# Replanning the opening of an attention and gated-linear-unit kernel: two load queues, weights first, single-step narrowing, two gates off VectorE

## The chip, the cores and the metric

The kernel runs on one core of a Trainium2 chip. The metric is the device time of one execution in microseconds, as the median of several runs. A profiled execution also gives a span, which is shorter than the time of that same execution by a constant 1.8 us; marks inside an execution are given on the span's clock. All comparisons are between runs that were classed as fast, unless it is said.

## The reference, cut to what matters

```python
kv  = einsum('bhsd,bhse->bhde', k, v)            # 8 batches, 8 heads, 576 rows, 64 wide
out = einsum('bhsd,bhde->bhse', q, kv)
x   = out / sqrt(mean(out*out, -1) + 1e-6) * g_norm    # then (B, S, 512)
gate = sigmoid(causal_conv(x, conv_w))           # 5 taps over time, per channel
val  = x @ w_val                                 # weights are float64 in the input
result = (gate * val) @ w_out
```

The weights arrive as 64-bit floats and have to be narrowed to 32 bits on the core. That costs seven VectorE instructions for each of eight blocks (four of `w_val`, four of `w_out`).

## The kernel before

Everything is emitted by steps with a planned time. The plan only sorts the steps. Each engine then runs its own instructions in that order and waits where data is missing. All large loads go through the sync queue (SP). An engine *issues* a load by an instruction of its own, and the load *lands* later.

```python
def raw_product(b, c):                   # one chunk of up to 128 rows, 5 chunks per batch
    raw = ps("raw", [P, C], ...)         # two PSUM banks
    ...
def scales(b, c):
    nc.vector.reduce_sum(out=ss, in_=sq.rearrange("p (h e) -> p h e", h=H), axis=AX.X)
    nc.gpsimd.tensor_scalar(out=ss, in0=ss, scalar1=D * EPS, ..., op0=ALU.add)
    nc.gpsimd.tensor_tensor(out=rt, in0=ss, in1=mhalf, op=ALU.pow)
def normalise(b, c):                     # x = raw * rt, frees the raw bank
    nc.vector.tensor_tensor(out=x, in0=raw, in1=rt, op=ALU.mult)
def gate_tap(b, jt, tap):                # 4 a gate, 4 gates a batch
    nc.vector.scalar_tensor_tensor(out=gate, in0=xT[shifted], scalar=cwT[...], in1=gate, ...)
def narrow(key, dst):                    # seven VectorE instructions in one go
    ...
# ---- plan of the opening (cut) ----
at(0.0, load_kv, 0, 0);  at(0.1, load_kv, 0, 1)      # k, v of batch 0
at(0.2, load_q_rows, 0, c)                           # 18 loads of 64 KB in short rows
at(0.3, stage_weight, "wval", jt)                    # three blocks of 512 KB
at(0.4, load_kv, 1, i)                               # k, v of batch 1
when[n] = 17.0 + 3.5 * n if n < NK else 32.0 + 4.0 * (n - NK)   # narrowings
```

Names used below: a *raw product* is q times kv for one chunk. *val* is x times `w_val` (eight groups of eight matmuls a batch), and *out* is the last product (four or five groups a batch). Four marks divide an execution: the first raw product, the first val, the first out of batch 0, and the first val of batch 1.

## Time and profile before

| | before |
|---|---|
| time, median (four runs in all) | 406.49 us (405.75 to 407.01) |
| span of the profiled execution (a further one, which took 407.68 us) | 405.9 us |
| PE busy, whole span | 358.3 us (88%) |
| VectorE busy, whole span | 231.8 us (57%) |
| first raw, first val, first out, val of batch 1 | 16.65, 50.09, 86.26, 114.70 us |
| from val of batch 1 to the end of the span | 291.2 us |

How to read it: a busy share over the whole span mixes two regimes. From 110 us on, TensorE is busy 97% of the time, and little but less work there can help. In the first 110 us every engine waits in turn, and what counts is how late each mark comes. The page's chain that ended last, by engine, says the same of the whole: mostly PE, then VectorE, then transfers.

```profile
PE 62%; DVE 16%; DMA 8%; SPq 5%; ACT 3%; POOL 3%; issue 3%; DVEq 0%; ACTq 0%
```

### The profile page before, as it was taken

The numbers are of one execution on the slowest core, as the hardware profiler recorded it, in microseconds if no ns is written. First come the engines' busy times: TensorE is split into PE (matmuls) and PEld (weight loads), VectorE is DVE, ScalarE is ACT, GpSimd is POOL, SyncE is SP. The second block draws the span as 40 slices with busy tenths as digits, with TensorE's granted clock in tenths as the row PEclk, the third lists the DMA queues.
The fourth block names the chain that finished last, engine by engine and source line by source line (L and its number), as shares of the span: only waits on it lengthen the run. The fifth ranks groups of instructions, "written<-read, shape, count | busy, mean of one in ns | idle before, by whom it ended". The sixth has DMA issues, their size and how long they took to land.

```text
span 405.9 us, 5359 instructions
## 1 busy us (share of the span) xinstructions
PE 358.3 (88%) x1961; PEld 238.9 (59%) x1961; DVE 231.8 (57%) x392; ACT 117.7 (29%) x192; POOL 98.7 (24%) x122
## 2 busy tenths in 40 slices
PE   1745596768998999999999999999999999999995
PEld 1644465534566764776477646774777467846742
DVE  3145888952259636665775376757663567555400
ACT  1112331013341234143412351335222523433011
POOL 2032600013300460165005500560045104610000
PEclk9997679869999899999999999999999999999999
DMA  7997430003969913791388135932782220022023
GB/s 186 171 313 220 122 103 2 0 0 97 257 194 246 235 27 78 178 275 34 78 239 214 34 79 143 279 91 67 178 248 74 67 65 0 1 53 52 0 52 78
DMA packets 49559, 49.00 MB, mean 121 GB/s; under 512 B 22890, under 2 KB 41342, under 8 KB 49534
## 3 DMA queue, kind: packets, MB, share of 16 engines
q1 hardware_dynamic: 49374, 48.67, 46.7%
q8 instruction: 15, 0.25, 0.3%
q14 instruction: 10, 0.08, 0.1%
q10 hardware_dynamic: 160, 0.00, 0.0%
HBM read 39.21 MB, written 9.44 MB: 120 GB/s over the span
## 4 chain that ended last, share of the span: by engine, by line
PE 62%; DVE 16%; DMA 8%; SPq 5%; ACT 3%; POOL 3%; issue 3%; DVEq 0%; ACTq 0%
PE out L367 25%; PE val L348 22%; PE raw L271 8%; DVE gate L336 5%; PE xTps L311 3%; PE kv L236 3%; DMA v<-in_v_dram 3%; DMA q<-in_q_dram 2%; POOL rt L293 2%; SPq L378 2%; DMA out_dram<-ot 2%; DMA w_wval<-in_moe_w_val_dram 1%; SPq L118 1%; DVE x L299 1%; SPq L149 1%
## 5 line engine op out<-in xcount | busy, mean ns | idle before, releaser
L348 PE MATMUL val<-xT,wval 128*128 128x288 f32 x512 | 141.1, 425 | 6.3 <-DVE gv L357 4.7
L367 PE MATMUL out<-wout,gv 128*128 128x512 f32 x288 | 129.3, 601 | 0.0
L348 PEld LDWEIGHTS val<-xT,wval 128*128 128x128 f32 x512 | 96.8, 196 | 35.0 <-DVE gv L357 5.6
L336 DVE SCALAR_TENSOR_TENSOR gate<-xT,cwT,gate 128x576 f32<-128x576 f32 x128 | 102.9, 810 | 21.2 <-ACT gate L330 19.3
L367 PEld LDWEIGHTS out<-wout,gv 128*128 128x128 f32 x288 | 53.9, 193 | 60.6 <-issue 59.8
L289 POOL TENSOR_SCALAR ss<-ss 128x8 f32<-128x8 f32 (+1 forms) x40 | 16.9, 423 | 253.6 <-DVE ss L286 253.6
L293 POOL TENSOR_TENSOR rt<-ss,mhalf 128x8 f32<-128x8 f32 (+1 forms) x40 | 70.0, 1750 | 3.3
L271 PE MATMUL raw<-kvbd,qT 128*128 128x128 f32 (+1 forms) x320 | 48.8, 301 | 22.7 <-DVE x L299 12.0
L271 PEld LDWEIGHTS raw<-kvbd,qT 128*128 128x128 f32 (+1 forms) x320 | 43.7, 198 | 32.9 <-issue 17.2
L299 DVE TENSOR_TENSOR x<-raw,rt 128x512 f32<-128x512 f32 (+1 forms) x40 | 27.6, 689 | 56.6 <-POOL rt L293 56.6
L280 ACT ACTIVATE sq<-raw 128x512 f32<-128x512 f32 (+1 forms) x40 | 23.8, 596 | 92.4 <-PE raw L271 92.4
L343 ACT ACTIVATE gate<-gate 128x576 f32<-128x576 f32 x32 | 21.9, 683 | 77.3 <-DVE gate L336 77.3
L286 DVE TENSOR_REDUCE ss<-sq 128x8 f32<-128x512 f32 (+1 forms) x40 | 27.1, 677 | 29.2 <-ACT sq L280 29.0
L357 DVE TENSOR_TENSOR gv<-val,gate 128x288 f32<-128x288 f32 x64 | 28.5, 451 | 18.6 <-PE val L348 15.9
L318 ACT ACTIVATE xT<-xTps,gcol 128x512 f32<-128x512 f32 (+1 forms) x40 | 25.3, 643 | 43.2 <-PE xTps L311 42.9
L375 ACT COPY ot<-out 128x512 f32<-128x512 f32 x36 | 21.0, 584 | 46.6 <-DMA out_dram<-ot 18.3
L236 PE MATMUL kv<-v,k 128*64 128x64 f32 x512 | 23.0, 242 | 9.2 <-DMA v<-in_v_dram 9.2
L236 PEld LDWEIGHTS kv<-v,k 128*64 128x64 f32 x512 | 19.9, 153 | 16.7 <-issue 14.8
L311 PE MATMUL xTps<-ident,x 128*128 128x128 f32 (+1 forms) x160 | 24.2, 279 | 3.9 <-DVE x L299 3.8
L311 PEld LDWEIGHTS xTps<-ident,x 128*128 128x128 f32 (+1 forms) x160 | 18.5, 148 | 13.3 <-issue 11.1
L330 ACT ACTIVATE gate<-xT,cwT 128x576 f32<-128x576 f32 x32 | 24.5, 771 | 0.2
L254 DVE STREAM_TRANSPOSE qT<-q 128x576 f32<-128x576 f32 x24 | 18.3, 768 | 0.0
(45 smaller groups left out, 92.9 us busy)
## 6 DMA issues: line engine op xcount, KB each, us to landing
q<-in_q_dram SPq DMA_DIRECT2D x96, 140.0 KB, 4.4
out_dram<-ot SPq DMA_DIRECT2D x144, 64.0 KB, 1.7
k<-in_k_dram SPq DMA_DIRECT2D x16, 512.0 KB, 7.2
v<-in_v_dram SPq DMA_DIRECT2D x16, 512.0 KB, 7.9
q<-in_q_dram SPq DMA_DIRECT2D x36, 64.0 KB, 2.6
w_wval<-in_moe_w_val_dram SPq DMA_DIRECT2D x4, 512.0 KB, 6.5
w_wout<-in_moe_w_out_dram SPq DMA_DIRECT2D x4, 512.0 KB, 3.4
kl<-in_k_dram SPq DMA_DIRECT2D x8, 128.0 KB, 6.3
```

Source lines behind the costliest of these rows:

```text
L236: nc.tensor.matmul(kvp[r * D:(r + 1) * D, hp, :], st["k", b, half][:, h, j, :] if j < NJ else kl[:, 2 * hp + r, :], st["v", b, half][:, h, ...
L271: nc.tensor.matmul(raw[0:m, hp * P:(hp + 1) * P], st["qT", b][:, hp, c * P:c * P + m], kv_bd[b % 2][:, hp, :], start=True, stop=True,)
L286: nc.vector.reduce_sum(out=ss[0:m], in_=st["sq", b, c][0:m].rearrange("p (h e) -> p h e", h=H), axis=AX.X,)
L293: nc.gpsimd.tensor_tensor(out=rt[0:m], in0=ss[0:m], in1=mhalf[0:m], op=ALU.pow)
L299: nc.vector.tensor_tensor(out=x[0:m].rearrange("p (h e) -> p h e", h=H), in0=st["raw", b, c][0:m].rearrange("p (h e) -> p h e", h=H), in1= ...
L311: nc.tensor.transpose(px[:, kc, 0:m], st["x", b, c][0:m, kc * P:(kc + 1) * P], ident[0:m, 0:m])
L318: nc.scalar.activation(out=xTs[b % 3][:, :, first:first + m], in_=st["px", b, c][:, :, 0:m], func=AF.Copy, scale=gcol[:],)
L330: nc.scalar.activation(out=gate[:], in_=xTs[b % 3][:, jt, HALO:SX], func=AF.Copy, scale=cwT[:, K - 1, jt:jt + 1])
L336: nc.vector.scalar_tensor_tensor(out=gate[:], in0=xTs[b % 3][:, jt, tap * TB:tap * TB + S], scalar=cwT[:, tap, jt:jt + 1], in1=gate[:], op ...
L348: nc.tensor.matmul(val[:], wval[:, kc, jt * P:(jt + 1) * P], xTs[b % 3][:, kc, HALO + n * SV:HALO + (n + 1) * SV], start=(kc == 0), stop=( ...
L357: nc.vector.tensor_tensor(out=gv[:, jt, first:first + SV], in0=st["val", b, jt, n][:], in1=st["gate", b, jt][:, n * SV:(n + 1) * SV], op=A ...
L367: nc.tensor.matmul(po[:], gv[:, jt, c * P:(c + 1) * P], wout[:, jt, :], start=(jt == 0), stop=(jt == NK - 1),)
```

## The change

The intent is to start the dense part sooner: weights come ahead of k and v so that VectorE can narrow them while it has nothing else to do; q goes through ScalarE's own queue; batch 0's raw products get five banks; narrowing steps are spread singly between other work; two of batch 0's gates are taken off VectorE; and the add of epsilon is folded into the sum as a 65th element. The diff, cut to its core:

```diff
+    sqs = [const.tile([P, H, D + 1], FP32, name=f"sq{i}") for i in range(2)]   # column D holds D*EPS
-    nc.vector.reduce_sum(out=ss[0:m], in_=st["sq", b, c][0:m].rearrange(...), axis=AX.X)
-    nc.gpsimd.tensor_scalar(out=ss[0:m], in0=ss[0:m], scalar1=D * EPS, ...)
+    nc.vector.reduce_sum(out=ss[0:m], in_=st["sq", b, c][0:m], axis=AX.X)
-    raw = ps("raw", [P, C], f"raw{b}_{c}")
+    raw = ps("mm" if b == 0 and c >= NJ - 2 else "raw", [P, C], f"raw{b}_{c}")
+    def gate_tap_aside(b, jt, tap):
+        nc.scalar.activation(out=prod[:], in_=xTs[...], func=AF.Copy, scale=cwT[:, tap, jt:jt + 1])
+        nc.gpsimd.tensor_tensor(out=gate[:], in0=gate[:], in1=prod[:], op=ALU.add)
...
+    at(0.0, stage_weight, "wval", 0)
+    for c in ORDER:
+        at(0.1, load_q_rows, nc.scalar, 0, c)
+    at(0.2, load_kv, 0, 0)
+    at(0.3, stage_weight, "wval", 1)
+    at(0.4, load_kv, 0, 1)
+    at(0.5, stage_weight, "wval", 2)
+    at(0.5, stage_weight, "wval", 3)
+    at(0.6, load_kv, 1, i)
...
+    gate(0, 0, 33.0, 0.8)
+    gate(0, 2, 33.1, 1.3, gate_tap_aside)
+    gate(0, 1, 36.3, 0.8)
+    gate(0, 3, 39.7, 1.3, gate_tap_aside)
+    mlp(0, 33.0, 61.0)
+    attention(1, 50.0, 2.4, 38.0, 47.5)      # batch 1's raw products ahead of batch 0's out products
```

## The prediction

> **What bounds the kernel now.** First I read the stretches (busy microseconds by engine, with instruction counts).
>
> ```profile
> core 0: us, PE busy (x) PEld busy (x) DVE busy (x) ACT busy (x) POOL busy (x), PEclk, DMA share, GB/s
> 20.00:30.00 10.00, 4.04 (x17) 3.67 (x18) 4.98 (x9) 1.48 (x3) 3.69 (x4) 1.00 1.10 310
> 40.00:50.00 10.00, 5.09 (x23) 3.73 (x21) 8.21 (x17) 3.54 (x6) 6.35 (x8) 0.67 0.52 131
> 50.00:60.00 10.00, 9.13 (x24) 6.43 (x24) 8.90 (x16) 3.81 (x6) 0.00 (x0) 0.69 0.31 105
> 60.00:70.00 10.00, 6.77 (x61) 5.26 (x62) 8.98 (x17) 1.65 (x3) 0.00 (x0) 1.00 0.01 2
> 70.00:80.00 10.00, 8.60 (x64) 5.86 (x62) 9.70 (x18) 0.68 (x1) 0.00 (x0) 0.83 0.00 0
> 110.00:406.00 296.00, 287.10 (x1559) 187.42 (x1557) 169.80 (x266) 92.94 (x153) 75.13 (x86) 0.99 0.45 116
> ```
>
> After 110 us PE is busy 287.1 of 296 us at clock 0.99: it is the bound there, and an opening change can't touch it much. Before that VectorE is the busy one, 8.2 to 9.7 of every 10 us from 40 to 80, and TensorE often runs at a granted clock near 0.68. So the loss is in the first 110 us. The timeline fixes the marks I carry through: the first raw product, the first val product, the first out product of batch 0, the first val product of batch 1.
>
> ```profile
> 16.65 1.97 PE L271 MATMUL raw<-kvbd,qT 128*64 128x128 f32 x8 [0.46 <-ACT qT L265]
> 50.09 9.13 PE L348 MATMUL val<-xT,wval 128*128 128x288 f32 x24 [0.78 <-ACT xT L318]
> 86.26 5.74 PE L367 MATMUL out<-wout,gv 128*128 128x512 f32 x8
> 114.70 4.15 PE L348 MATMUL val<-xT,wval 128*128 128x288 f32 x16 [0.78 <-ACT xT L318]
> ```
>
> From batch 1's val to the end is 406.35 - 114.70 = 291.65 us, and I take that as fixed. Why do the marks come so late? Among the waits of PE and VectorE up to 115 us:
>
> ```profile
> PE raw L271 <- DVE x L299: 10.4, 3, 5.6
> PE kv L236 <- DMA v<-in_v_dram: 9.2, 2, 7.9
> PE val L348 <- DVE gv L357: 4.7, 4, 3.0
> DVE wexp_wval L178 <- DMA w_wval<-in_moe_w_val_dram: 3.6, 1, 3.6
> ```
>
> Only two raw banks exist, so raw c must wait until VectorE has made x of c+2; and VectorE stands behind a weight narrowing that itself waits for its weights, which the queue issued only after the 18 q loads:
>
> ```profile
> 6.09 12.30 SPq L149 DMA_DIRECT2D q<-in_q_dram  x18
> 18.43 1.55 SPq L163 DMA_DIRECT2D w_wval<-in_moe_w_val_dram  x3
> 23.57 0.43 DVE L178 TENSOR_SCALAR wexp_wval<-w_wval 128x512 uint32<-128x512 uint32 x1 [3.61 <-DMA w_wval<-in_moe_w_val_dram]
> ```
>
> Last, the transfer rate in 40 slices of the first 60 us (1.5 us each):
>
> ```profile
> GB/s 0 60 310 235 265 148 326 285 176 157 139 134 129 201 358 363 351 349 267 209 272 352 237 34 221 256 185 126 138 136 110 306 14 0 63 287 0 183 167 0
> ```
>
> k, v and weights move at 235 to 360 GB/s, but q, in its short rows, at about 135 (slices 10 to 13), with the DMA engines still full. This decides what loading weights first costs.
>
> **What the Trainium skill says.** "DMA: Bandwidth & Descriptors", Issuing engines are not separate DMA queues: loads issued by several engines run on the same 16 engines and interleave; only issue time is saved. The trace has one load queue, so it can't confirm it; the engines being full agrees with it. "SBUF — State Buffer", SBUF: two separate sides: VectorE operations with two SBUF inputs, or in a two-port mode, and GpSimd operations exclude each other for the whole instruction. The trace agrees in part: four halo copies on GpSimd take 2.58 us beside a narrowing (42.25) and 0.99 alone (106.23), yet VectorE loses only about 0.1 us there. "GPSIMD Engine Reference", Elementwise — side-by-side cycle accounting: an add of two tensors needs about 2.6 cycles an element at 1.2 GHz. No such add of this size is in the trace; 576 x 2.6 / 1.2 = 1.25 us is an estimate, 1.35 with a start-up. "TensorE: Matmul & The Clock Gate", Part 1: The HAM clock gate: after a few idle microseconds the clock halves. The trace agrees in kind: eight val matmuls take 3.04 us at 68.69 and 2.21 at 77.08.
>
> **The change, part by part.**
>
> *Loads.* Until kv is whole, the new queues move k and v (2.25 MB), two blocks of wval (1.0 MB) and, beside them, q (1.15 MB). At some 265 GB/s and 135 GB/s that is 12.3 + 8.5 = 20.8 us after a start at 2.3, or 23 us, if q takes its whole share first; about 18 if q lags on its queue. I choose 21 for the landing of the second half of v, against 13.17 before. Then PE has two kv pairs (1.55 each) and a q turn (1.06), 4.2 us, and VectorE the kv copy (0.86): the first raw product starts at about **26**, that is 9 us *later* than before.
>
> *Five banks for batch 0's raw products and the earlier weights.* They remove the 10.4 and 3.6 us of waits, and the first two narrowings (2 x 3.8 = 7.6 us) move into the time in which VectorE waited for kv. From the first raw end (28) and its square (0.6), VectorE has in order 5 sums (0.68), 5 scalings (0.69) and ten narrowing steps (7 of block 2 are 3.85, 3 of block 3 are 1.3): 3.4 + 3.45 + 5.15 = 12.0 us, to 40.6, as it is nearly never without work; add 0.8 for waits on rt and 1.8 for turn and copy of x: first val at **43.2**, 6.9 us before the old 50.1.
>
> *Val phase.* VectorE's queue from there to the last narrowing of wout, which the first out product needs: 4 steps of block 3 (2.5), 8 taps instead of 16 (8 x 0.83 = 6.6), 8 gated products (8 x 0.45 = 3.6), kv copy of batch 1 (0.86), 28 narrowing steps (4 x 3.8 = 15.2), three sums and two scalings of batch 1 (3.4): 32.2 us, starting at 41.4: 73.6. To this come lock waits: 8 GpSimd adds, each holding VectorE for at most 1.2 us, 9.6 us at worst; I take half, 4.8 us, as products from PSUM, single-input sums and gaps can lie beside them. PE needs val 8 x 2.2 = 17.6, kv 3, q turns 2.5, raw 5.5, x turns 1.2, in all 30 us warm, so 43 + 30 = 73: no earlier than VectorE. ScalarE's 8 products (8 x 0.76 = 6.1 us) fit, but the sigmoid of gate 1 stands in its queue behind that of gate 2, hence behind four GpSimd adds: I give 1.6 us of stall. First out product at 73.6 + 4.8 + 1.6 = **80** (before: 86.3).
>
> *Out and batch 1.* Before, batch 1's attention stood mostly between and after the four out products: 114.70 - 86.26 = 28.4 us. Now its q turns and raw products lie earlier, and behind the first out product PE has 4 x 3.5 = 14 us of out and three x turns (1.8): 15.8, so val of batch 1 at **95.8** against 114.7, a gain of 18.9 us.
>
> *Steady state.* One GpSimd add fewer for each of 40 chunks (16.9 us of GpSimd busy time) and a shorter path from square to x. PE is the bound there, and has only 9 us of idle time in 296; I give 1 us gain. Against it: batch 2's k, v and q are issued behind the first store, about 80 + 4, only 12 us ahead of val of batch 1, where before they were 114.7 - 97.7 = 17 us ahead: 2 us of new wait. The sum is 406.35 - 18.9 - 1 + 2 = 388.5. As the kv landing could well be nearer 18, which takes up to 3 us off, I put the point at **387**.
>
> **Rivals.** (a) *Transfers are the bound*: weights first only push kv and q back, and the first val product comes no earlier than 50. For it: engines full from 3 to 21 us, and 8 us of q transfer interleaved. Against it: in the old opening val did not wait for data after 24 us, but for VectorE. Then only the val phase and the batch 1 overlap gain, 12 us: 394. (b) *GpSimd becomes the bound of the val phase*: adds slowed like the halo copies, 2.58 / 0.99 = 2.6 times, take 1.35 x 2.6 = 3.5 us, eight of them 28 us after 47: gate 3 would be ready only at 75, and ScalarE copies no q of batch 1 before, so out comes some 15 us after that, at 90, val of batch 1 at 106: 397. For it: the slowed copies; against it: VectorE has waits of its own in which adds run. (c) *Everything fits as planned*, kv whole at 15 and adds hidden: first val at 38, out at 68, val of batch 1 at 84: 375. (d) A new stall behind batch 2's loads of 6 us or more: 392.
>
> **Range and chances.** The point is the chain of marks, with half the lock cost. (c) is the low side; (a), (b) and (d) the high side, and only two of them together come over 398, the 2% line. Range 376 to 396; faster by over 2% 0.90, within 2% 0.09, slower 0.01.
>
> **What would show each step right or wrong.** First raw product at 24 to 28 (later than 16.65), with PE's wait on DMA v grown; PE's wait for x before raw gone; first val at 40 to 46; GpSimd adds of 1.3 to 2 us, with taps and narrowing steps beside them lengthened or preceded by gaps; first out at 76 to 84; val of batch 1 at 92 to 99; after it PE busy over 97% as before. The prediction is wrong if val of batch 1 comes after 103 (GpSimd or loads bind), or if the tail from that mark differs from 291.65 us by over 4.

## The result, and the profile after

| | before | after |
|---|---|---|
| time, median | 406.49 us (4 runs) | 400.66 us (4 runs, 399.75 to 401.8) |
| ratio of the means, 95% interval | | 0.9859 (0.9825 to 0.9894) |
| first raw product | 16.65 | 38.42 |
| first val product | 50.09 | 53.45 |
| first out product | 86.26 | 96.59 |
| val of batch 1 | 114.70 | 111.64 |
| from there to the end of the span | 291.2 | 286.3 |

A ratio here is the mean time of one kernel's fast runs over that of the other's of the same rounds, so it is not quite the ratio of the medians that are quoted. The change gains 1.4%, which is within 2%; the forecast was 387 us with a range of 376 to 396.

The marks of the changed kernel in its timeline (start and duration in us, then engine, line, operation, operands, count, and in brackets the idle time before and what ended it):

```profile
38.42 3.96 PE L286 MATMUL raw<-kvbd,qT 128*64 128x128 f32 x32
53.45 7.90 PE L371 MATMUL val<-xT,wval 128*128 128x288 f32 x24 [0.78 <-ACT xT L331]
...
96.59 3.60 PE L390 MATMUL out<-wout,gv 128*128 128x512 f32 x8
...
111.64 4.04 PE L371 MATMUL val<-xT,wval 128*128 128x288 f32 x16
```

The first raw product is more than twice as late as before. Three of the four marks are later than before, and only the last is earlier, by 3.1 us. The rest, 4.9 us, comes after it. Beware of that rest: these two executions lie 8.0 us apart and the medians only 5.8, as the profiled execution before (407.68 us) was slower than the four timed ones and the one after (399.75 us) was the fastest of its four. The stretches of the changed kernel (columns as in the prediction):

```profile
20.00:30.00 10.00, 1.33 (x20) 1.15 (x20) 0.47 (x1) 0.00 (x0) 0.00 (x0) 1.00 1.19 267
...
60.00:70.00 10.00, 10.00 (x110) 7.63 (x108) 9.89 (x12) 5.28 (x8) 5.64 (x4) 1.00 0.01 2
70.00:80.00 10.00, 8.00 (x49) 6.34 (x48) 9.72 (x17) 3.51 (x7) 3.35 (x3) 1.00 0.00 0
80.00:90.00 10.00, 3.50 (x18) 2.94 (x17) 7.97 (x17) 2.02 (x4) 3.85 (x2) 0.72 0.01 2
```

From 20 to 30 us almost nothing computes (PE 1.33 us, VectorE 0.47, ScalarE nothing) while the transfer engines are full. From 60 to 80 VectorE is full again. From 80 to 90 PE is down to 3.5 us. So there are two separate losses. The chain that ended last, by engine, and its first pieces in order of time, show the first:

```profile
PE 64%; DMA 14%; DVE 10%; issue 3%; ACT 3%; SPq 2%; POOL 2%; ACTq 0%; DVEq 0%; POOLq 0%
```

```profile
1.97 6.84 DMA q<-in_q_dram
8.84 7.88 DMA q<-in_q_dram
17.09 7.09 DMA q<-in_q_dram
24.20 6.57 DMA q<-in_q_dram
30.79 6.93 DMA q<-in_q_dram
```

The share of transfers in that chain grew from 8% to 14%, and from 1.97 to 37.7 us it consists of q loads only. What holds q on its way? These lines are the wait of ScalarE (total, times, longest) and the issue of q on ScalarE's queue:

```profile
ACT L280 <- DMA q<-in_q_dram: 31.1, 1, 31.1
```

```profile
1.97 29.14 ACTq L155 DMA_DIRECT2D q<-in_q_dram  x18
```

The same 18 issues took 12.30 us on the sync queue before. Now they take 29.14, and ScalarE can copy no transposed q until the last is out, as its own instruction stream contains them. The two queues between 12 and 20 us (packets, MB, share of 16 engines' time), first the kernel before, where q has the engines to itself:

```profile
q1 hardware_dynamic: 4647, 1.15, 88.4%
```

and the changed kernel, where q is q10:

```profile
q1 hardware_dynamic: 1885, 1.85, 95.7%
q10 hardware_dynamic: 1117, 0.27, 17.7%
```

In the same 8 us q gets 0.27 MB instead of 1.15, while the sync queue carries 1.85 MB of data, part of which is wanted only much later (wval blocks 2 and 3, then k and v of batch 1).

One more thing makes the mark wait for the whole of q. Before, each raw product stood behind its own turn of q on PE (turns at 15.51 and 18.55 us, raw products at 16.65 and 20.34). The new plan puts all five turns of batch 0 (planned at 9.1 to 16.7) ahead of the first raw product (17.0), so that it comes at 38.42, right behind the last turn at 37.85, which waited for the last q load. No run changes this order alone.

### The profile page after: what moved, and what is told of

Same layout as the page of the kernel before. It is cut to its first block, busy times and chain, and to the rows that moved or that the text cites. A ratio compares the mean times of both kernels' runs of the same rounds, so it can differ in the third digit from the quotient of the medians.

```text
span 397.9 us, 5362 instructions
## 1 busy us (share of the span) xinstructions
PE 346.9 (87%) x1961; PEld 232.7 (58%) x1961; DVE 233.9 (59%) x386; ACT 123.3 (31%) x200; POOL 98.5 (25%) x90
## 4 chain that ended last, share of the span: by engine, by line
PE 64%; DMA 14%; DVE 10%; issue 3%; ACT 3%; SPq 2%; POOL 2%; ACTq 0%; DVEq 0%; POOLq 0%
PE out L390 25%; PE val L371 24%; DMA q<-in_q_dram 11%; PE raw L286 8%; PE xTps L324 4%; PE kv L251 3%; DVE gate L349 2%; POOL rt L306 2%; DMA out_dram<-ot 2%; DMA k<-in_k_dram 2%; SPq L401 2%; DVE x L312 1%; DVE ss L304 1%; DVE wmf_wout L211 1%; ACT ot L398 1%
## 5 line engine op out<-in xcount | busy, mean ns | idle before, releaser
L371 PE MATMUL val<-xT,wval 128*128 128x288 f32 x512 | 137.2, 416 | 1.3 <-ACT xT L331 0.8
L306 POOL TENSOR_TENSOR rt<-ss,mhalf 128x8 f32<-128x8 f32 (+1 forms) x40 | 75.0, 1877 | 239.1 <-DVE ss L304 239.0
L390 PE MATMUL out<-wout,gv 128*128 128x512 f32 x288 | 127.0, 593 | 0.0
L349 DVE SCALAR_TENSOR_TENSOR gate<-xT,cwT,gate 128x576 f32<-128x576 f32 x120 | 100.0, 844 | 29.7 <-ACT gate L343 27.9
L371 PEld LDWEIGHTS val<-xT,wval 128*128 128x128 f32 x512 | 94.8, 192 | 28.6 <-issue 2.7
L296 ACT ACTIVATE sq<-raw 128x512 f32<-128x512 f32 (+1 forms) x40 | 23.9, 596 | 103.4 <-PE raw L286 103.4
L286 PE MATMUL raw<-kvbd,qT 128*128 128x128 f32 (+1 forms) x320 | 44.6, 285 | 11.3 <-DVE x L312 9.1
L286 PEld LDWEIGHTS raw<-kvbd,qT 128*128 128x128 f32 (+1 forms) x320 | 40.8, 187 | 19.7 <-issue 10.1
L304 DVE TENSOR_REDUCE ss<-sq 128x8 f32<-128x520 f32 (+1 forms) x40 | 27.5, 686 | 27.6 <-ACT sq L296 27.3
L261 DVE COPY kvbd<-kv 64x256 f32<-64x256 f32 x16 | 6.6, 416 | 24.3 <-PE kv L251 24.2
L278 PE MATMUL qTps<-ident,q 128*128 128x128 f32 (+1 forms) x40 | 8.0, 339 | 12.5 <-ACT qT L280 10.6
```

The source lines that it names most:

```text
L286: nc.tensor.matmul(raw[0:m, hp * P:(hp + 1) * P], st["qT", b][:, hp, c * P:c * P + m], kv_bd[b % 2][:, hp, :], start=True, stop=True,)
L304: nc.vector.reduce_sum(out=ss[0:m], in_=st["sq", b, c][0:m], axis=AX.X)
L306: nc.gpsimd.tensor_tensor(out=rt[0:m], in0=ss[0:m], in1=mhalf[0:m], op=ALU.pow)
L349: nc.vector.scalar_tensor_tensor(out=gate[:], in0=xTs[b % 3][:, jt, tap * TB:tap * TB + S], scalar=cwT[:, tap, jt:jt + 1], in1=gate[:], op ...
L371: nc.tensor.matmul(val[:], wval[:, kc, jt * P:(jt + 1) * P], xTs[b % 3][:, kc, HALO + n * SV:HALO + (n + 1) * SV], start=(kc == 0), stop=( ...
L390: nc.tensor.matmul(po[:], gv[:, jt, c * P:(c + 1) * P], wout[:, jt, :], start=(jt == 0), stop=(jt == NK - 1),)
```

## The experiments

My theory was that q on its own queue loses the transfer engines to data that is not wanted yet, and that this, not the computing, sets the first 38 us. The main rival was that VectorE's queue of work sets the later marks anyway, so that q's lateness hardly matters. The experiments ran in three groups on three chips, each beside its own runs of the kernel before (medians 405.12, 405.96 and 405.85 us). All results were correct.

### 1. q back on the sync queue

```diff
-        at(0.1, load_q_rows, nc.scalar, 0, c)
+        at(0.45, load_q_rows, nc.sync, 0, c)
```

> The changed kernel with batch 0's 18 q loads back on the first queue, behind batch 0's k and v and the second wval block and ahead of the other two wval blocks and batch 1's k and v. Theory A (on its own queue, q shares the transfer engines with data that nothing needs yet and so lands at 37.85 us, holding ScalarE's first copy to 32 us): the first raw product comes at 24 to 27 us instead of 38.4, the first val product at 40 to 44 instead of 53.5, and the end 8 to 12 us sooner than the changed kernel (389 to 393 us). Rival (VectorE's queue of narrowing and taps sets the later marks anyway): the first raw product moves, but batch 1's first val product moves by less than 4 us and the time stays at 397 to 401.

Measured: 388.19 us (386.0 to 391.59), ratio 0.9576 (0.9513 to 0.9638). The marks:

```profile
24.70 3.96 PE L286 MATMUL raw<-kvbd,qT 128*64 128x128 f32 x32
...
39.74 7.87 PE L371 MATMUL val<-xT,wval 128*128 128x288 f32 x24 [0.78 <-ACT xT L331]
...
82.88 3.60 PE L390 MATMUL out<-wout,gv 128*128 128x512 f32 x8
...
97.93 4.04 PE L371 MATMUL val<-xT,wval 128*128 128x288 f32 x16
```

In the profiled executions all four marks come 13.7 us sooner than in the changed kernel, and so does the end (span 384.2 against 397.9). By the ratios of all runs the gain is 11.5 us (0.0283 of 406); the profiled execution is the fastest of the four. The rival is out: q's way to the core sets the opening. The lateness of q passes undiminished through everything behind it, because each later stage keeps its length. The edit undoes two things at once, though: q's sharing of the transfer engines, and the hold on ScalarE by its own issues. Groups 2 and 3 look at them apart.

### 2. q still on ScalarE's queue, batch 1's k and v later

```diff
-        at(0.6, load_kv, 1, i)
+        at(15.1, load_kv, 1, i)
```

> The changed kernel, q still issued by ScalarE, but batch 1's k and v (2.25 MB) are issued behind the second wout block, so after 20 us. Theory A (the loads compete): ScalarE's q issues, which took 29.1 us, end at 20 to 25 us, the first raw product comes at 27 to 32 us, and the time falls by 4 to 9 us against the changed kernel. Rival (ScalarE's queue is slow in itself, some 1.6 us an issue): the issues still take 27 to 30 us and the first raw product stays at 37 to 39.

Measured: 395.79 us, ratio 0.9765 (0.9722 to 0.9808), so 3.8 us below the changed kernel (0.0094 of 406). The issues end at 28.5 us, and the first raw product comes at 34.50. The direction is theory A's, but each number is short of its window. From 12 to 20 us q gets 0.27 MB as before, beside 1.71 MB of the sync queue: in that stretch the wval blocks and batch 0's own k and v still go beside it, and from 18.92 us on a block of wout in place of batch 1's k.

### 3. Is ScalarE's queue slow in itself? A quiet sync queue

One staging buffer instead of four, later weight loads placed behind the narrowing that frees it, and batch 1's loads behind the second block:

```diff
-        t = loads.tile([P, C, 2], U32, tag="w64", bufs=4, ...)
+        t = loads.tile([P, C, 2], U32, tag="w64", bufs=1, ...)
-    at(0.0, stage_weight, "wval", 0)
+    at(4.3, stage_weight, "wval", 0)
...
-        at(0.6, load_kv, 1, i)
+        at(14.2, load_kv, 1, i)
```

> The changed kernel, q still issued by ScalarE, but the first queue kept quiet behind batch 0's k and v: one staging buffer instead of four, so each weight block is issued only when the one before is narrowed, and batch 1's k and v behind the second block. A look at the opening only; the later weights come late on purpose. Theory A (q loses to what the first queue carries beside it): ScalarE's 18 issues end at 16 to 22 us instead of 31.1. Rival (ScalarE's queue is slow in itself): they still end at 27 to 31.

Measured (one run of 412.03 us, its state unknown; the later weights come late on purpose): the last issue ends at 25.7 us, which is between the two windows. The detail helps more. Between 16 and 18 us, when the sync queue has little left, q runs at 0.33 MB in 2 us, 165 GB/s, more than the 0.27 MB it got in 8 us of the changed kernel:

```profile
q10 hardware_dynamic: 1363, 0.33, 100.0%
```

By 19.1 us 15 of the 18 issues are out. The last three come only here:

```profile
24.40 1.32 ACTq L155 DMA_DIRECT2D q<-in_q_dram  x3
```

So the queue is not slow in itself; it is slow beside another one. But from 20 to 22 us the q queue used 14.2% of the engines and the sync queue nothing, and still no issue went out. They went out half a microsecond after a wval block, which the sync queue carried from 22 to 23.9 us; whether that held them is not shown and stays open. The hold on ScalarE is a cost of its own here: PE waits 9.04 us for ScalarE's first copy, until 27.47, and the first raw product comes at 31.59, against 24.70 in q_on_sync.

### 4. All of batch 0's taps on VectorE

```diff
-    gate(0, 2, 33.1, 1.3, gate_tap_aside)
+    gate(0, 2, 33.1, 1.3)
-    gate(0, 3, 39.7, 1.3, gate_tap_aside)
+    gate(0, 3, 39.7, 1.3)
```

> The changed kernel with all of batch 0's taps on VectorE again (8 more taps of 0.83 us, 6.6 us), nothing on GpSimd. Theory (a GpSimd add and a VectorE instruction with SBUF operands exclude each other, so the 8 adds stretched VectorE's taps and narrowing steps by about 8 us in all): VectorE's taps and narrowing steps go back to 0.83 and 0.42 to 0.69 us each, the first out product comes within 2 us of the changed kernel's 96.6, and the time is within 2.5 us of it. Rival (the offload frees VectorE as intended): the first out product comes 5 to 7 us later and the time rises by 4 to 7 us.

Measured: 401.37 us, ratio 0.9890 (0.9854 to 0.9926), against 0.9859 of the changed kernel, so the same within the intervals. The first out product comes at 96.68 against 96.59, though this run's first raw product was 1.3 us later. The offload buys nothing measurable. In the changed kernel the taps from 54 to 74 us (count, then busy time and mean ns), and VectorE's narrowing steps beside the adds of gate 3 in the timeline, look like this:

```profile
L349 DVE SCALAR_TENSOR_TENSOR gate<-xT,cwT,gate 128x576 f32<-128x576 f32 x8 | 10.4, 1313 | 0.5 <-ACT gate L343 0.3
...
66.94 6.58 POOL L362 TENSOR_TENSOR gate<-gate,prod 128x576 f32<-128x576 f32 x4 [4.02 <-ACT prod L358]
67.05 1.84 DVE L201 SCALAR_TENSOR_TENSOR wexp_wout<-w_wout,wexp_wout 128x512 uint32<-128x512 uint32 x1
...
68.81 1.63 DVE L206 TENSOR_SCALAR wman_wout<-w_wout 128x512 uint32<-128x512 uint32 x1
```

and without the adds the same groups are, with their mean in ns after the busy time:

```profile
L349 DVE SCALAR_TENSOR_TENSOR gate<-xT,cwT,gate 128x576 f32<-128x576 f32 x16 | 12.4, 814 | 0.4 <-ACT gate L343 0.3
L201 DVE SCALAR_TENSOR_TENSOR wexp_wout<-w_wout,wexp_wout 128x512 uint32<-128x512 uint32 x4 | 2.7, 686 | 0.1
...
L206 DVE TENSOR_SCALAR wman_wout<-w_wout 128x512 uint32<-128x512 uint32 x4 | 1.7, 419 | 0.0
```

A step of 0.42 us became 1.63. In the stretch from 54 to 74 us, eight taps took 1.313 us on the mean instead of 0.814 (4.0 us more), and four narrowing steps 6.77 us in all instead of 2.47 (4.3 more). The eight adds, 1.65 us each and 13.2 in all, thus cost VectorE 8.3 us to save 8 x 0.814 = 6.5 us of taps.

The same with q out of the way, gate by gate:

```diff
-    gate(0, 2, 33.1, 1.3, gate_tap_aside)
+    gate(0, 2, 39.6, 0.8)
-    gate(0, 3, 39.7, 1.3, gate_tap_aside)
+    gate(0, 3, 42.9, 0.8)
```

> q on the first queue as in q_on_sync and all taps of batch 0 on VectorE, gate by gate (0, 1, 2, 3) as before the change. If GpSimd's adds gain nothing because they hold VectorE off: within 2.5 us of q_on_sync (ratio to the kernel before 0.952 to 0.964), the first out product within 2 us of 82.9. If the offload helps once q is out of the way: 4 to 7 us slower than q_on_sync.

Measured: 386.09 us, ratio 0.9499 (0.9466 to 0.9532), first out at 81.99 against 82.88. It is 3 us better than q_on_sync by the ratios, slightly below the expected window, but the two intervals touch and the profiled spans are equal (384.2). So it is not the 4 to 7 us slower that the rival expected. The order of gates 1 and 2 changed with it.

### 5. Two banks again

```diff
-        raw = ps("mm" if b == 0 and c >= NJ - 2 else "raw", [P, C], ...)     # on q_on_sync
+        raw = ps("raw", [P, C], ...)
```

> q_on_sync with batch 0's raw products on two banks again. If the extra banks are worth their share: the third raw product waits for x (in the kernel before these waits were 10.4 us in all), PE waits for x again by 4 to 10 us, and the first val product comes 2 to 5 us later than 39.7, and the time 2 to 5 us above q_on_sync. If VectorE's chain of sums, scalings and narrowing steps sets the pace anyway: PE waits, but the first val product moves by less than 1.5 us.

Measured: ratio 0.9681 (0.9640 to 0.9723; 394.07 us is the median of four runs, one of them slow). The first val product comes at 46.68 instead of 39.74. PE's wait for x ahead of raw products grew from 8.7 us to

```profile
PE raw L286 <- DVE x L312: 16.9, 6, 6.5
```

The five banks are worth about 4.3 us of time (0.0105 of 406). At the first val mark they are worth more than I expected, 6.9 us.

### 6. Narrowing in one go

```diff
-            at(first + n * step, narrow_weight, *key, n)     # on q_on_sync
+            at(first, narrow_weight, *key, n)
```

> q_on_sync with each weight block narrowed in one go, seven instructions together, instead of in single steps among the others. The first two blocks are narrowed while VectorE waits for data, so nothing changes there. If the single steps matter: a whole block (3.8 us) stands ahead of sums and scalings, the first val product comes 1 to 4 us later than 39.7 and the time is 2 to 5 us above q_on_sync. If VectorE's total work sets the pace, order inside it does not matter: first val within 1 us, the time within 2 us of q_on_sync.

Measured: 394.71 us, ratio 0.9718 (0.9676 to 0.9759). The first val product comes at 44.95 and the val of batch 1 at 106.82. Single steps are worth about 5.8 us (0.0142 of 406), a little above the window, and the first val product is 5.2 us later than in q_on_sync, also above it; 1.4 of the 5.2 are there already at the first raw product (26.07 against 24.70), where PE waited for q until 18.89 us instead of 17.46. In this trace a whole block stands on VectorE between the first sum of a chunk (27.82) and the second (32.20). So order inside the engine mattered, though its total work was the same.

### 7. The folded epsilon alone, on the kernel before

```diff
-        nc.scalar.activation(out=sq[0:m], in_=st["raw", b, c][0:m], func=AF.Square)      # on the kernel before
+        nc.scalar.activation(out=sq[0:m, :, 0:D], in_=st["raw", b, c][0:m].rearrange(...), func=AF.Square)
...
-        nc.gpsimd.tensor_scalar(out=ss[0:m], in0=ss[0:m], scalar1=D * EPS, scalar2=None, op0=ALU.add)
```

> The kernel before with only the padded square (the epsilon as a ninth... 65th summand instead of an add on GpSimd for each of 40 chunks). The changed kernel's stretch from batch 1's first val product to the end is 286.3 us against 291.2 before. If the pad is what shortened it: that stretch is 287 to 289 us here, and the whole time is 3 to 6 us below before's. If the shorter stretch comes from how the opening hands over (clock, work done earlier): the stretch stays at 290 to 291.5 and the time falls by 0 to 2 us, the hops saved in the opening.

Measured: 402.70 us, ratio 0.9922 (0.9876 to 0.9969), about 3 us. From val of batch 1 (112.15) to the end of the span (398.8) is 286.65 us, against 291.2 before and 286.3 in the changed kernel. The steady state itself shows it in the chain that ended last, in two blocks of 24 out matmuls that are one pair of batches apart:

```profile
186.60 10.30 PE out L369 x24
...
268.90 10.30 PE out L369 x24
```

The pair takes 82.30 us here. It took 83.43 in the kernel before (191.44 to 274.87) and 82.73 in the changed one (184.87 to 267.60). So the fold shortens a pair by 1.13 us, some 3 us over the three pairs of the tail. The rest of the tail's 4.55 us is not the fold's. In both kernels PE waits 1.74 us for batch 2's kv, and the 16 val matmuls behind that wait took 5.84 us in the profiled execution before but 4.15 in this one:

```profile
130.80 5.84 PE L348 MATMUL val<-xT,wval 128*128 128x288 f32 x16
...
128.25 4.15 PE L350 MATMUL val<-xT,wval 128*128 128x288 f32 x16
```

The granted clock was 0.59 to 0.78 there and 1.00 here, after the same wait. The fold's whole-time gain came out at the lower end of what was expected, and this kernel's four runs spread over 3.7 us.

### 8. Batch 1's raw products among the out products

```diff
-    attention(1, 50.0, 2.4, 38.0, 47.5)                   # on q_sync_taps
+    attention(1, 54.0, 3.6, 38.0, 49.0, late=1.5)
-    mlp(0, 33.0, 61.0)
+    mlp(0, 33.0, 58.0)
-        gate(1, jt, 68.0 + 4.0 * jt, 0.8)
+        gate(1, jt, 77.2 + 4.0 * jt, 0.8)
-    begin = 61.0 + NJ * DO
+    begin = 77.0
```

> q_sync_taps with batch 1's raw products spread among batch 0's out products instead of standing ahead of the first. In the changed kernel PE waited 8.7 us for x ahead of raw products, 6.5 of it ahead of the first out product. If that order is what holds the first out product: it comes at 74 to 79 us instead of about 83, batch 1's first val product 2 to 5 us sooner, the time 2 to 5 us below q_sync_taps. If VectorE's narrowing of wout holds it: the out product moves by under 3 us and the time by under 2.

Measured: 383.64 us (381.52 to 383.88), ratio 0.9424 (0.9386 to 0.9463), the best of all: 5.8% below the kernel before and 4.4% below the changed one (0.9424 / 0.9859). The val of batch 1 comes at 94.82 instead of 97.58. My marker for the first out product failed. PE starts it at 65.22, far before the window, and then stands in the middle of it for the narrowing of `w_out`:

```profile
PE out L390 <- DVE wout L215: 4.0, 2, 3.0
```

So both causes that I had set against each other hold: the order, with the times of batch 1's gates and val that the edit moves along with it, cost about 3 us by the ratios, and behind it VectorE's narrowing still binds.

One step further, with the chunks closer together (2.9 instead of 3.6 units, gates and val sooner by 2.9 and 1.2):

> raw1_spread with batch 1's chunks 2.9 instead of 3.6 units apart, and its gates and val 1.2 to 2.9 units sooner. In raw1_spread VectorE waited 10.2 us for rt in this stretch, since each sum stands behind the scaling of the chunk before. If the sums now run a chunk ahead: that wait falls to 2 to 6 us, batch 1's first val product comes 1 to 3 us sooner than 94.8, and the time falls by 1 to 3 us. If two raw banks chain them anyway: no change beyond 1 us.

Measured: 387.15 us, ratio 0.9537 (0.9521 to 0.9553), slower than raw1_spread by 1.2% (0.9537 / 0.9424, each against its own runs of the kernel before). VectorE's wait for rt did fall, from 10.2 to 2.9 us, but its wait for the squares grew from 6.5 to 11.3; the val of batch 1 came 0.5 us sooner, at 94.28, and the tail grew from 287.0 to 290.1 us. Behind the val of batch 1 PE waits longer for batch 2's kv (2.79 us against 1.27), and after that wait the next two val groups run slowly:

```profile
111.43 5.84 PE L371 MATMUL val<-xT,wval 128*128 128x288 f32 x16
```

In raw1_spread the same 16 matmuls take 4.15 us. The granted clock of this stretch is 0.76 to 0.77 here and 1.00 there. The longer wait (1.5 us) and the slow matmuls (1.7 us) make 3.2 us, which is the 3.1 us by which the tail grew in these two executions. As the same wait was followed by a low clock in one kernel and not in another (group 7), the slow matmuls may belong to this execution and not to the edit.

## Why the prediction was wrong

Faster by over 2% was wrong, and the time lies 4.7 us above the range. Step by step:

**First raw product, predicted 26, measured 38.42: the step that failed.** The landing of v was right: PE waited for it until 20.95 us, and I had chosen 21. What failed is the clause that everything lands in 23 us "if q takes its whole share first; about 18 if q lags on its queue". I treated q's lag as a gain for k and v and forgot that q is needed as well. I counted only the bytes ahead of v, not those that a second queue lets in beside q, and not that ScalarE is held while its issues wait: it copied no turned q before 32.44 us. I also counted one q turn behind v where the plan has PE make all five before the first raw product. With q on the sync queue the mark is 24.70, in spite of that order. Rival (a), transfers as the bound, had the right kind of cause, and put the time at 394.

**Raw to first val, predicted 17.2 us, measured 15.0** in the changed kernel and in q_on_sync alike. The bank experiment and the one-go narrowing show that the five banks and the single steps are both needed; no run tests the earlier weights alone.

**First val to first out, predicted 36.8 us, measured 43.1** in both (96.59 - 53.45, 82.88 - 39.74). Here a term was mis-sized: I took half of the worst lock cost, 4.8 of 9.6 us, and the adds cost 8.3 of their own 13.2. Gaps and PSUM products absorbed less of it than I assumed. A second term was missing: batch 1's raw products stand ahead of the first out product on PE and wait for x there, up to 6.5 us at once. How much each is worth in this stretch does not follow exactly from the runs, as taking the adds away puts the taps back. Rival (b) was wrong in its mechanism: the adds took 1.65 us and not 3.5 (my estimate for one alone was 1.25 to 1.35, and none ran alone); it was they that slowed VectorE.

**Out to val of batch 1, predicted 15.8, measured 15.05.** Right.

**The tail, taken as fixed but for +1 us, measured 4.9 us shorter.** The mechanism was named, the shorter path from square to x, but sized at 1 us. Before the change PE waited 1.74 us for batch 2's kv and then ran 16 val matmuls in 5.84 us at a clock as low as 0.59. The changed kernel waits 0.71 and runs them in 4.15. That is 2.7 us, but 1.7 of it, the slow matmuls, cannot be credited to the change: before_pad keeps the 1.74 us wait and runs them in 4.15. A pair of batches is shorter by 0.70, which over three pairs gives some 2 more. So about 3 of the 4.9 us are shown to be the change's, and the rest is luck of the two executions. The new stall of 2 us behind batch 2's loads did not come.

Together, against the prediction's own sum, 388.5 before it was rounded to 387, put on the span's clock (95.8 + 291.2 + 1 = 388.0; I had taken the tail as 291.65, a median time less a mark of another, slower execution): +12.4 - 2.2 + 6.3 - 0.7 - 5.9 = +9.9, which is the measured 397.9. With the one failed step undone (q_on_sync, 388.19 us) the forecast of 387 would have held, partly by luck, because the error in the val phase and that in the tail cancel.

So where did the expected gain go? On q, 11.5 us were lost by the ratios (13.7 between the profiled executions), and about 8 us of VectorE time to the adds, which gave up what they saved. The fold of epsilon gave about 3 us (1.3 to 5.0 by the interval of before_pad) of the 5.7 that the change gained in all.

## What to carry to other kernels

A second load queue was not extra bandwidth here: by the rates of the stretches, the first 40 us moved 8.96 MB before, 8.98 with two queues and 9.02 with q back on one. Before splitting loads, ask which transfer the first consumer needs last and what the other queue will put beside it, and don't let an engine issue loads that it must itself wait behind. Before moving elementwise work from VectorE to GpSimd, look whether VectorE is full beside it: here it was, and the move gained nothing. Follow a late mark through the later stages: if each keeps its length, one early microsecond is worth a microsecond at the end.

## What the Trainium skill lacked or had wrong

- "DMA: Bandwidth & Descriptors", Issuing engines are not separate DMA queues: the page is right that nothing is gained in bandwidth, but it calls the issue time, the one thing that a second issuer saves, "usually small relative to the DMA itself". Here the 18 issues held ScalarE for 29.14 us, against 12.30 us on the one queue; one such load took 6.7 us to land (median).
- No page that I found has it: three issues on ScalarE's queue were held from 19.1 to 24.4 us, while nothing at all moved from 20.7 to 22.0 us; no run here explains it.
- "SBUF — State Buffer", SBUF: two separate sides: nothing wrong was found, as the exclusive lock that it describes fits the numbers. Eight adds cost VectorE 8.3 us, about 1.04 us each of their 1.65. In the kernel before it was GpSimd that was held, for four short copies (2.58 us against 0.99), and VectorE lost 0.1 us.
- "TensorE: Matmul & The Clock Gate", Part 1: The HAM clock gate: the page's table has the clock fall after an idle window of about 3.4 us. Here it fell after shorter waits of PE, of 1.74 us (before), 2.17 (q_act_quiet) and 2.79 (raw1_closer), to 0.59 to 0.78 in the stretches behind them, but not after 1.74 us in before_pad or 1.64 in q_sync_2banks, where the same 16 matmuls took 4.15 us. The length of the last wait alone does not decide it.
